# Half of w_in moved into the last stage, a first token block of 512, and a new attention order in a fused attention and soft-MoE kernel

## The chip, the cores and the metric

One core of a Trainium2 chip runs the whole program in one launch. The metric is the device time of one execution in microseconds, as the median over runs. The profile shows one further execution, and its own time is given beside its span.

## The reference

```python
attn = softmax(rmsnorm(q) @ rmsnorm(k).T / 8) @ v      # 4 batches, 12 heads, 448 tokens, 64 wide
x = attn as [1792, 768]
logits = x @ phi                                       # phi [768, 32]: 8 experts of 4 slots
d = softmax(logits, over tokens); slot_input = d.T @ x # [32, 768]
slot_out[e] = relu(slot_input[e] @ w1[e]) @ w2[e]      # w1 [8, 768, 1024], w2 [8, 1024, 768]
x = softmax(logits, over slots) @ slot_out             # [1792, 768]
h = x @ w_in                                           # w_in [768, 2048], float64 in memory
out = (h * sigmoid(1.702 * h)) @ w_out                 # w_out [2048, 768], float64 in memory
```

## The kernel before

The kernel has three stages.

**Attention.** 24 pairs of heads pass through a pipeline whose steps are listed with `op(name, engine, cost, due, function, needs, ...)`. `run` is a planner: it plays the list with its costs and emits each engine's instructions in the order that comes out. Where several steps of one engine could start at the same time, the one with the smallest due goes first. `SHIFT` adds a number to the due of each kind of step, and the strings in `ON` say for each pair whether a step runs on VectorE (D), GpSimd (P) or ScalarE (A). While attention runs, 24 pieces of expert weights are loaded ahead (`early`). They fill seven tiles of 128x3072: `NW` = 3 of `wpool`, which are loaded again later, and 4 that lie in `wi`, the place of the decoded w_in, and are not. At the end of attention five more tiles are filled (`ev`, `e0` to `e3`).

**Experts.** Eight experts follow each other. For each one TensorE computes `hps` = siT x w1 (line 1121, six steps of kk), VectorE applies the ReLU (`hs`, line 1134), TensorE turns it (line 1144), VectorE copies it into `hTz` (lines 1149, 1150), and TensorE multiplies it by w2 into `so_ps` (line 1154, eight steps of f, for the first six experts). A tile of weights that has been used is filled again with the next one of the list `stream` (`reload`, on SyncE's queue). From the sixth expert on `warm_b` adds dummy products. In the second expert `combine_turn` prepares the combine weights; for the first batch it also keeps a plain copy `c0` for the first tokens. After each step of the loops `win_turn` may decode one chunk of w_in: 24 chunks of 128x512 float64 values, 0.524 MB each, are loaded by ScalarE's queue (`win_load`, line 1043) and turned into float32 by `decode64` with two steps on ScalarE (lines 147, 150) and two on VectorE (line 144). The w2 of the last two experts come last in `stream` and are used by `last_mm` (line 1232). `u_step` (line 1261) multiplies their sum `before` by w_in, which gives `u`, the 32 slots' values in all 2048 features.

**Last stage.** Tokens are worked off in blocks, and a planner orders it too. For each of 16 feature tiles f, `f_mm` spreads `ust` to the tokens (line 1310), ScalarE applies Silu (`gg`, line 1318) and rounds it (`gh`, line 1327), VectorE takes the rest (`gl`, line 1332), and TensorE adds three products for each token tile of 128 and each half of 768 columns into `Y`: gh x wh, gh x wl, gl x wh (line 1351; in the first block line 1368). `us_mm` (line 1291) makes `ust` from `u` in four parts. In the first block the 16 tiles of w_out are loaded, decoded and split into `wh` and `wl` as well (lines 144 to 158, 1210, 1214). The blocks are 384, 384, 384, 384 and 256 tokens; `y_out` and `y_store` write a finished block.

Of the kernel before, what the change touches and what calls it, by code (L numbers as in the profile page):

```python
# [20 lines left out]
def soft_moe_block_kernel(  # L21
# [29 lines left out]
    NW, NWR, NW2 = 3, 4, 2  # L51
# [3 lines left out]
        gain="PDPDPDDDPDDPDPDPDDPDDDDD",  # L55
        qn="DPPDPPPPPPDPPPDPPPPPDPDD",
        kn="DPDDDPPPPPDDPPDPPPDDPDPP",
        qlo="PPDPPPDPDDPPDDPPDPDDPPPD",
        klo="DDDDDDPPPDPDDPDDDPDPDPDD",
        q2="PPDAAADAPDDDDDAAAAPDPPDA",  # L60
        k2="DDDADDADADPDADAAADPAADPA",
        e01="PPDPDPDPPPPPDDDPDDDPDPDP",
        e02="PPDPPPPPPDDDPPPPDDDDDPPD",
        e11="DPPPDDPPPPDDDPDDDDDDPDPP",
        e12="PPDDDPPPPDPDDPPDDDPPDDPD",
        x0="DDDDAAADADDDDAADAADAADDA",
        x1="DAAAADDAADADDADAADDADAAA",
        nr="DPPDPDPPDPDP",
# [96 lines left out]
    wi = wi_ctx.__enter__().tile([128, KD * DFF], F32, name="wi")  # L165
# [55 lines left out]
    for i, tag in enumerate(("ssq", "y0", "nt")):  # L221
# [42 lines left out]
        e0=4065.4, e1=1871.6, e2=705.9, e3=1336.9, early=76.2, esum=1946.8, ev=1170.2, exp=938.3, gain=3568,  # L264
        guard=-7.4, invert=-243.4, k2=1786.8, khi=-2180.8, klo=-680.2, kn=1837.3, lastlg=-2574.3, lk=1816.2,
        lk2=3100.6, logits=522.6, lq=1423.8, lq2=582.8, max=1121.1, meansq=1101.5, mx=-29, out=798.9,
        pe_tka=-2476.8, pe_tkb=3670.2, pe_tqa=681.5, pe_tqb=-366.9, pv=510.7, q2=1966, qhi=3834, qlo=1235.4,
        qn=1990.6, r_add=3872.4, r_back=3899.1, r_eb=1801, r_exp=-2634.4, r_fade=1302.1, r_gather=624.9,
        r_max=1791.5, r_more=-2250.9, r_neg=1305.5, r_old=1619.3, r_turn=681.3, r_z=352.5, recip=1344.9,
        sc=586, square=-471.5, squarek=473, ssb=-536.7, sumT=1332.9, sums=-8.9, tka=-2650.5, tka0=719.8,  # L270
        tkb=3875.6, tkb0=-229.5, tqa=-2002, tqa0=523.6, tqb=-542.8, tqb0=1302.7, v=4133.3, w_back=1921.6,
        w_copy=1410.9, w_exp=1561, w_guard=-358.8, w_max=-206.5, w_neg=-343.2, w_recip=-2399.9, w_scale=1149.9,
        w_sel=3867.1, w_sum=581.9, w_turn=1912.7, w_z=3874.4, x=2168.9, xmul=1473.5,
# [385 lines left out]
    for p in range(NP):  # L659
# [40 lines left out]
        if p >= NPE:  # L700
            op(("tka", p), "SP", 1.32, t - 16.3, lambda p=p: turn(p, "kt", KT, kk_t), sub("klo", "k2"), ("kt", p), [("ka", p)])
# [256 lines left out]
    left += [f for i in range(4) for f in place(wi[:, 3072 * i:3072 * (i + 1)], None)]  # L958
# [19 lines left out]
    with tc.manual_schedule():  # L978
# [26 lines left out]
        for h in range(2):  # L1005
# [23 lines left out]
            for i in range(6)  # L1029
# [17 lines left out]
        def win_turn():  # L1047
# [20 lines left out]

        def combine():
# [11 lines left out]
        def combine_turn(b):  # L1081
# [25 lines left out]
        c0 = bp.tile([NS, SF], F32, name="c0")  # L1107
# [61 lines left out]
        QU = DFF // 4  # L1169
# [3 lines left out]
        FB = dict(h=2, hs=2, wr=5, wf=4, gg=3, gh=4, gl=4, o=3, y0=1, y1=1, y2=1)  # L1173
# [19 lines left out]
        def w_step(f, i, h):  # L1193
# [3 lines left out]
            decode64(wf[f][:, c], wr[f][:, 2 * c.start:2 * c.stop], f % 2)[i]()  # L1197
# [58 lines left out]
        def u_step(kk):  # L1256
            if kk == 0:
                st["u"] = ps_o.tile([128, QU], F32, tag="o", name="u")
            for j in range(4):
                a = kk * DFF + j * QU  # L1260
# [10 lines left out]

        def u_hi():
            nc.scalar.activation(out=uh, in_=st["u"], func=AF.Copy)

        def u_lo():
            nc.vector.tensor_tensor(out=ul, in0=st["u"], in1=uh.bitcast(F32), op=ALU.subtract)

        def close():
# [4 lines left out]
            cp["ust"] = poolf("us", 1).tile([128, DFF], F32R, name="ust")  # L1283
            for t in FB:
                if t not in cp and t[0] not in "hy":
                    cp[t] = poolf(t + "_q", FB[t] - 3 * (t in right))

        def us_mm(j):
            st["us", j] = ps_h.tile([128, 512], F32, tag="h", name="f")
            for hl, t in ((0, uh), (1, ul)):  # L1290
                nc.tensor.matmul(
                    st["us", j], selu[:, j, hl].rearrange("p t s -> p (t s)"), t, start=(hl == 0), stop=(hl == 1)
                )
# [237 lines left out]
```

## Time and profile before

| what | value |
|---|---|
| median of 3 runs | 690.77 us (690.19 to 692.08) |
| the profiled execution's own time | 688.41 us |
| its span, first to last instruction | 686.6 us |
| TensorE busy | 617.3 us (90%) |
| VectorE busy | 396.3 us (58%) |
| ScalarE busy | 364.3 us (53%) |
| GpSimd busy | 164.5 us (24%) |

PE is TensorE, PEld its weight loads, DVE VectorE, ACT ScalarE, POOL GpSimd, SP SyncE; a q behind the name is the queue that issues transfers. L1154 is line 1154 of the kernel. The shares are means over the three stages, which have different limits, so they have to be read stage by stage.

### The profile page before, as it was taken

Reading aid. Unit: us, or ns where it says so; the run is one execution under the profiler, and the core shown is the slowest. Engines: PE = TensorE matmul, PEld = TensorE weight load, DVE = VectorE, ACT = ScalarE, POOL = GpSimd, SP = SyncE. Lnnn points to the kernel's source line nnn. Section 1 sums busy time; section 2 is a strip of 40 time slices with the busy share of each in tenths; the row PEclk is TensorE's granted clock in tenths of the full one; section 3 lists DMA queues with packets and bytes.
Section 4 is the critical chain, followed back from the end, with each engine's and each line's share of the span. In section 5 each row is a group of like instructions: output and inputs, shape, how many; then the busy total and the mean of one; then the engine's idle time right before and its main releaser. Section 6 shows DMA issues by size and latency. Waiting matters only on the chain.

```text
span 686.6 us, 10997 instructions
## 1 busy us (share of the span) xinstructions
PE 617.3 (90%) x4104; PEld 414.0 (60%) x4104; DVE 396.3 (58%) x657; ACT 364.3 (53%) x756; POOL 164.5 (24%) x193
## 2 busy tenths in 40 slices
PE   2989998999999999986743999999999999999997
PEld 1434343344444343453421344999899999999997
DVE  5978988898899997354444514899401211211211
ACT  4757787769768675643334412897413323432432
POOL 4565775873562551300000200000000000000000
PEclk9999999999999999999876999999999999999999
DMA  8989999998999999689899994761100100100101
GB/s 215 289 162 209 194 198 206 183 181 184 194 185 190 210 227 214 209 321 353 322 407 405 406 349 178 266 232 72 70 1 0 70 1 1 70 0 1 70 1 46
DMA packets 150965, 121.73 MB, mean 177 GB/s; under 512 B 106848, under 2 KB 131680, under 8 KB 150912
## 3 DMA queue, kind: packets, MB, share of 16 engines
q1 hardware_dynamic: 147824, 110.91, 59.7%
q10 hardware_dynamic: 3024, 10.03, 3.8%
q8 instruction: 32, 0.52, 0.3%
q14 instruction: 21, 0.17, 0.1%
q0 software_dynamic: 64, 0.10, 0.1%
HBM read 92.18 MB, written 5.51 MB: 142 GB/s over the span
## 4 chain that ended last, share of the span: by engine, by line
PE 67%; DMA 12%; DVE 11%; ACT 4%; issue 3%; POOL 3%; SPq 1%; ACTq 0%; DVEq 0%; POOLq 0%
PE y L1351 27%; PE y L1368 7%; PE sc L545 6%; PE pv L564 4%; PE so_ps L1154 4%; DVE wr L534 3%; DMA wr<-wr 3%; PE mx L529 2%; DMA wr<-in_q_dram 2%; PE h L1121 2%; PE f L1310 2%; DMA wr<-in_moe_w_dram 2%; DVE wr L417 1%; PE t L1113 1%; PE pv L559 1%
## 5 line engine op out<-in xcount | busy, mean ns | idle before, releaser
L1332 DVE TENSOR_TENSOR gl<-gg,gh 128x384 fp32r<-128x384 f32 (+1 forms) x80 | 42.2, 530 | 154.0 <-ACT gh L1327 153.2
L534 DVE TENSOR_REDUCE wr<-mx 128x2 f16<-128x896 f32 x92 | 99.8, 1085 | 16.1 <-PE mx L529 16.0
L1318 ACT ACTIVATE gg<-f 128x384 f32<-128x384 f32 (+1 forms) x78 | 36.4, 468 | 116.8 <-PE f L1310 115.4
L1351 PE MATMUL y<-wo,gh 128*128 128x384 f32 x352 | 75.3, 335 | 0.0
L549 ACT ACTIVATE e<-sc,esc 128x448 f32<-128x448 f32 x96 | 58.0, 642 | 12.2 <-PE sc L545 8.8
L1351 PEld LDWEIGHTS y<-wo,gh 128*128 128x128 f32 x352 | 62.1, 188 | 0.0
L552 POOL TENSOR_TENSOR es<-es,e 128x448 f32<-128x448 f32 x36 | 44.1, 1236 | 50.6 <-PE pv L564 31.6
L545 PE MATMUL sc<-wr 128*128 128x448 f16 (+1 forms) x192 | 49.0, 365 | 2.2 <-DMA wr<-wr 1.7
L1327 ACT ACTIVATE gh<-gg 128x384 fp32r<-128x384 f32 (+1 forms) x78 | 39.3, 504 | 16.3 <-PE y L1351 10.7
L1351 PE MATMUL y<-wh,gl 128*128 128x384 f32 x176 | 46.8, 337 | 0.0
L1351 PE MATMUL y<-wh,gh 128*128 128x384 f32 x176 | 46.7, 336 | 0.0
L1351 PE MATMUL y<-wl,gh 128*128 128x384 f32 x176 | 46.7, 336 | 0.0
L549 ACT ACTIVATE es<-sc,esc 128x448 f32<-128x448 f32 x54 | 33.5, 642 | 21.6 <-PE sc L545 21.4
L1351 PE MATMUL y<-wo,gl 128*128 128x384 f32 x176 | 44.8, 335 | 0.0
L412 ACT ACTIVATE wr<-wr 128x512 f32<-128x512 f32 x48 | 30.6, 644 | 15.8 <-DMA wr<-in_k_dram 4.8
L472 POOL TENSOR_TENSOR wr<-wr 128x512 f32<-128x512 f32 x31 | 34.6, 1134 | 11.6 <-DVE wr L448 7.8
L545 PEld LDWEIGHTS <-wr 128*128 128x128 f16 (+1 forms) x256 | 19.0, 103 | 30.1 <-issue 21.3
L147 ACT ACTIVATE wi<-wst 128x512 f32<-128x512 f32 x24 | 16.2, 674 | 36.5 <-DMA wr<-in_moe_w_dram 16.1
L144 DVE SCALAR_TENSOR_TENSOR wst<-wst 128x512 uint32<-128x512 uint32 x24 | 16.6, 690 | 29.2 <-ACT wst L150 27.3
L1351 PEld LDWEIGHTS y<-wl,gh 128*128 128x128 f32 x176 | 32.0, 188 | 0.0
L1351 PEld LDWEIGHTS y<-wh,gl 128*128 128x128 f32 x176 | 32.0, 188 | 0.0
L1351 PEld LDWEIGHTS y<-wo,gl 128*128 128x128 f32 x176 | 31.9, 188 | 0.0
(264 smaller groups left out, 1324.6 us busy)
## 6 DMA issues: line engine op xcount, KB each, us to landing
wr<-in_moe_w_dram SPq DMA_DIRECT2D x30, 512.0 KB, 8.8
wt<-in_moe_w_dram SPq DMA_DIRECT2D x24, 512.0 KB, 7.8
wr<-in_moe_w_out_dram SPq DMA_DIRECT2D x15, 768.0 KB, 4.3
wst<-in_moe_w_in_dram ACTq DMA_DIRECT2D x19, 512.0 KB, 6.9
wt<-in_moe_w_dram SPq DMA_DIRECT2D x20, 384.0 KB, 7.8
wr<-in_moe_w_dram SPq DMA_DIRECT2D x20, 384.0 KB, 5.7
out_dram<-o SPq DMA_DIRECT2D x13, 384.0 KB, 2.3
wr<-in_k_dram SPq DMA_DIRECT2D x11, 384.0 KB, 5.1
```

What stands on the lines that cost most here:

```text
L412: nc.scalar.activation(out=sqt[p][:, 8 * i:8 * i + 8], in_=rows(p, i), func=AF.Square, scale=D ** -0.5)
L472: eng.tensor_tensor(out=n, in0=n, in1=r.to_broadcast([P, 8, D]), op=ALU.mult)
L534: nc.vector.tensor_reduce(out=lanes(of(qb_t, p), 1)[:m, h:h + n, c, 0:1], in_=MX.pop((p, g))[:m, :n, :S], axis=AX.X, op=ALU.max,)
L545: nc.tensor.matmul(out, cols(a, n, c), cols(b, n), start=first, stop=not first)
L549: nc.scalar.activation(out=E[p, h, c], in_=SC.pop((p, h, c)), func=AF.Exp, scale=esc)
L552: on(f"e{h}{c}", p)[0].tensor_tensor(out=E[p, h, 0], in0=E[p, h, 0], in1=E[p, h, c], op=ALU.add)
L564: nc.tensor.matmul(PV[p][h * D:(h + 1) * D, :], t[:, 6 * n + 3 * h + c], E[p, h, c], start=(c == 0), stop=False)
L1318: nc.scalar.activation(out=ggt[w][:, :w[1]], in_=src[:, :w[1]], func=AF.Silu, scale=1.702)
L1327: nc.scalar.activation(out=gh[:, :w[1]], in_=ggt[w][:, :w[1]], func=AF.Copy)
L1332: nc.vector.tensor_tensor(out=G[w][1][:, :n], in0=ggt[w][:, :n], in1=G[w][0][:, :n].bitcast(F32), op=ALU.subtract)
L1351: nc.tensor.matmul(Y[t, u][:, :384], a[:, ts], b[f][:, u * 384:(u + 1) * 384], start=(f == 0 and i == 0), stop=(f == KF - 1 and i == 2),)
L1368: nc.tensor.matmul(Y[t, u][:, :384], a[:, t * 128:(t + 1) * 128], b[:, u * 384:(u + 1) * 384], start=(f == 0 and j == 0), stop=(f == KF - ...
```

## The change

- Only the first 1024 columns of w_in (12 chunks) are loaded and decoded in the experts' stage, one each 5.2 turns from turn 21 on, four loaded ahead at the start and then three ahead. `wi` is half as large; in the place that comes free `wpool` has five tiles instead of three.
- The other 1024 columns (groups g = 2 and 3, six chunks each) are loaded by SyncE's queue in the last stage, decoded into `wx` by the same four steps (`late_load`, `late_step`), multiplied by a kept copy of `before` (`late_u`) and split (`late_hi`, `late_lo`). `us_mm` for parts 2 and 3 works from these.
- Blocks are 512, 512, 384 and 384 tokens. The columns of `Y` are divided as 512 + 256; the 256-column parts of two token tiles share one bank, which a product with zeros opens (`y_tile`).
- In w_out, four of 16 tiles instead of eight take the decode with three VectorE steps (`f % 4`). Rings: wr 5 to 4, wf 4 to 3, gg 3 to 2, gl 4 to 3.
- All strings of `ON` and numbers of `SHIFT` are new, and `SHIFT` also has kinds of the last stage. The planner's cost of the step `tka` is 2.9 instead of 1.32.

```diff
-    NW, NWR, NW2 = 3, 4, 2
+    NW, NWR, NW2 = 5, 4, 2
-        gain="PDPDPDDDPDDPDPDPDDPDDDDD",
+        gain="DDPDDDDDPDDDDDDDDPDDDDPD",
...
-        if is_kept[key] is not None and nstream[0] < len(stream) - (0 if is_kept[key] else NW):
+        if is_kept[key] is not None and nstream[0] < len(stream) - (0 if is_kept[key] else 3):
...
-    wi = wi_ctx.__enter__().tile([128, KD * DFF], F32, name="wi")
+    wi = wi_ctx.__enter__().tile([128, KD * DFF // 2], F32, name="wi")
...
-    left += [f for i in range(4) for f in place(wi[:, 3072 * i:3072 * (i + 1)], None)]
+    left += [f for i in range(2) for f in place(wi[:, 3072 * i:3072 * (i + 1)], None)]
...
-        NC, NWI = 512, KD * DFF // 512
+        NC, NWI = 512, KD * DFF // 1024
...
-            kc, col = divmod(j * NC, DFF)
+            kc, col = j // 2, j % 2 * NC
...
-            if j < NWI and g >= 16 + 2.75 * j:
-                if 0 < j < NWI - 4:
-                    win_load(j + 4, nc.scalar)
+            if j < NWI and g >= 21 + 5.2 * j:
+                if 0 < j < NWI - 3:
+                    win_load(j + 3, nc.scalar)
...
-        for j in range(5):
+        for j in range(4):
             win_load(j, nc.sync)
...
-        QU = DFF // 4
+        QU = DFF // 8
...
-        FB = dict(h=2, hs=2, wr=5, wf=4, gg=3, gh=4, gl=4, o=3, y0=1, y1=1, y2=1)
+        FB = dict(h=2, hs=2, wr=4, wf=3, gg=2, gh=4, gl=3, o=3, ws=2)
...
-            decode64(wf[f][:, c], wr[f][:, 2 * c.start:2 * c.stop], f % 2)[i]()
+            decode64(wf[f][:, c], wr[f][:, 2 * c.start:2 * c.stop], f % 4)[i]()
...
+        def late_load(g, kk):
+            st["ws", g, kk] = cp["ws"].tile([128, 2 * NC], U32, tag="ws", name="ws")
+            nc.sync.dma_start(
+                out=st["ws", g, kk], in_=win64[kk * 128:(kk + 1) * 128, 2 * g * NC:2 * (g + 1) * NC]
+            )
+
+        def late_step(g, kk, i):
+            a = kk * NC
+            decode64(cp["wx"][:, a:a + NC], st["ws", g, kk], True)[i]()
+
+        def late_u(g):
+            st["lu", g] = ps_h.tile([128, 512], F32, tag="h", name="f")
+            for kk in range(KD):
+                for j in range(4):
+                    a = kk * NC + 128 * j
+                    nc.tensor.matmul(
+                        st["lu", g][32 * j:32 * j + 32, :128], keep[:, kk % 2, kk // 2], cp["wx"][:, a:a + 128],
+                        start=(kk == 0), stop=(kk == KD - 1),
+                    )
...
+            parts, n = ((uh, ul), QU) if j < 2 else ((st["luh", j], st["lul", j]), 128)
+            for i in range(512 // n):
+                r = i + 2 * j if j < 2 else i
+                for hl, t in enumerate(parts):
+                    nc.tensor.matmul(
+                        st["us", j][:, i * n:(i + 1) * n], selu[:, r, hl].rearrange("p t s -> p (t s)"), t,
+                        start=(hl == 0), stop=(hl == 1),
+                    )
...
+        YC = (slice(0, 512), slice(512, DM))
+
         def y_tile(t, u):
-            ps, tag = (ps_c, "c") if t < 2 else ((ps_t, "t"), (ps_o, "o"))[u]
-            Y[t, u] = ps.tile([128, 512], F32, tag=tag, name="y")
+            if u == 0:
+                Y[t, 0] = ps_c.tile([128, 512], F32, tag="c", name="y")
+            elif t % 2 == 0:
+                ps, tag = ((ps_t, "t"), (ps_o, "o"))[t // 2]
+                pair = ps.tile([128, 512], F32, tag=tag, name="y")
+                Y[t, 1], Y[t + 1, 1] = pair[:, :256], pair[:, 256:]
+
+                some = ident.bitcast(F16).rearrange("p (o f) -> p o f", o=1).to_broadcast([128, 2, 256])
+                nc.tensor.matmul(pair, zeros, some, start=True, stop=False)
...
-                    Y[t, u][:, :384], a[:, ts], b[f][:, u * 384:(u + 1) * 384],
-                    start=(f == 0 and i == 0), stop=(f == KF - 1 and i == 2),
+                    Y[t, u], a[:, ts], b[f][:, YC[u]], start=(f == 0 and i == 0 and not u),
+                    stop=(f == KF - 1 and i == 2 and (u == 0 or t % 2 == 1 or (t + 1) * 128 == w[1])),
...
-        blocks = [(t0, min(384, NT - t0)) for t0 in range(0, NT, 384)]
+        blocks = [(0, T0), (T0, 512), (T0 + 512, 384), (T0 + 896, 384)]
...
-                        [("fhi", w), ("flo", w)] + ([("y", (w[0], n, f - 1), t)] if f else []),
+                        [("fhi", w), ("flo", w)] + ([("y", (w[0], n, f - 1), t)] if f else [("yo", prev, i, u) for i in (t, t1) if i < prev[1] // 128 for u in range(2)]),
```

## Rows read from the trace of the kernel before

**Rows 1.** Busy time by stage (us, instructions), then granted clock, DMA share, GB/s.

```profile
core 0: us, PE busy (x) PEld busy (x) DVE busy (x) ACT busy (x) POOL busy (x), PEclk, DMA share, GB/s
45.00:302.10 257.10, 243.75 (x1423) 104.85 (x1423) 215.66 (x325) 184.66 (x418) 133.58 (x129) 1.00 0.94 203
302.10:330.10 28.00, 21.43 (x255) 11.66 (x255) 14.34 (x37) 11.60 (x23) 0.57 (x2) 0.94 0.90 334
330.10:379.60 49.50, 25.97 (x296) 13.02 (x299) 22.71 (x40) 19.34 (x33) 0.00 (x0) 0.72 1.02 398
379.60:408.00 28.40, 26.97 (x277) 9.77 (x270) 8.86 (x20) 7.27 (x17) 3.93 (x17) 1.00 1.05 379
...
429.60:487.20 57.60, 57.19 (x315) 56.52 (x316) 51.85 (x71) 48.07 (x78) 0.00 (x0) 0.97 0.46 167
489.85:682.50 192.65, 192.62 (x1111) 192.30 (x1110) 36.49 (x70) 61.35 (x129) 0.00 (x0) 1.00 0.07 25
```

**Rows 2.** Waits from 330 to 380 us: total us, times, longest.

```profile
PE t L1144 <- DVE hTz L1149: 22.7, 3, 11.1
```

**Rows 3.** Timeline of ScalarE and VectorE before the fifth expert's ReLU.

```profile
360.80 0.69 ACT L147 ACTIVATE wi<-wst 128x512 f32<-128x512 f32 x1 [7.13 <-DMA wr<-in_moe_w_dram]
...
372.16 0.69 DVE L144 SCALAR_TENSOR_TENSOR wi<-wi,wst 128x512 uint32<-128x512 uint32 x1
372.77 0.48 DVE L1134 TENSOR_SCALAR hs<-h,rz 128x256 f32<-128x256 f32 x1
```

**Rows 4.** DMA traffic in 322 to 333, 333 to 360, 395 to 413 us.

```profile
DMA packets 670, 2.46 MB, mean 224 GB/s; under 512 B 69, under 2 KB 69, under 8 KB 670
...
DMA packets 3277, 10.91 MB, mean 404 GB/s; under 512 B 365, under 2 KB 365, under 8 KB 3275
...
DMA packets 6109, 6.31 MB, mean 351 GB/s; under 512 B 194, under 2 KB 6000, under 8 KB 6108
```

**Rows 5.** Waits of SyncE's queue from 295 to 420 us.

```profile
SPq L115 <- PE so_ps L1154: 10.2, 1, 10.2
```

**Rows 6.** Timeline of TensorE in the experts' stage (start, duration).

```profile
327.64 1.93 PE L1154 MATMUL so_ps<-wr,hTz 128*32 128x256 f32 x24
...
336.87 5.12 PE L1154 MATMUL so_ps<-wr,hTz 128*32 128x256 f32 x45 [0.28 <-DVE hTz L1150]
...
373.30 0.69 PE L1144 MATMUL t<-ident,hs 128*128 128x128 f32 x2 [11.07 <-DVE hTz L1149]
...
380.32 0.50 PE L1113 MATMUL t<-ident 128*128 128x256 f16 x3
```

**Rows 7.** Timeline of TensorE: the last products of the last experts.

```profile
422.33 1.08 PE L1232 MATMUL h<-wr,hTz 128*32 128x128 f32 x32
```

**Rows 8.** Timeline of TensorE in the last stage: starts of 512, 384, 256 columns.

```profile
439.02 0.39 PE L1291 MATMUL f<-uh,selu 128*128 128x512 f32 x1
439.25 0.40 PE L1291 MATMUL f<-ul,selu 128*128 128x512 f32 x1
...
530.33 0.51 PE L1351 MATMUL y<-wh,gh 128*128 128x384 f32 x2
530.67 0.51 PE L1351 MATMUL y<-wl,gh 128*128 128x384 f32 x2
...
660.36 0.28 PE L1310 MATMUL f<-cT,ust 128*128 128x256 f32 x1
660.48 0.87 PE L1351 MATMUL y<-wo,gh 128*128 128x384 f32 x4
```

**Rows 9.** Costliest groups of the whole run: busy us, mean ns.

```profile
L1332 DVE TENSOR_TENSOR gl<-gg,gh 128x384 fp32r<-128x384 f32 (+1 forms) x80 | 42.2, 530 | 154.0 <-ACT gh L1327 153.2
L1318 ACT ACTIVATE gg<-f 128x384 f32<-128x384 f32 (+1 forms) x78 | 36.4, 468 | 116.8 <-PE f L1310 115.4
...
L1327 ACT ACTIVATE gh<-gg 128x384 fp32r<-128x384 f32 (+1 forms) x78 | 39.3, 504 | 16.3 <-PE y L1351 10.7
...
L147 ACT ACTIVATE wi<-wst 128x512 f32<-128x512 f32 x24 | 16.2, 674 | 36.5 <-DMA wr<-in_moe_w_dram 16.1
L144 DVE SCALAR_TENSOR_TENSOR wst<-wst 128x512 uint32<-128x512 uint32 x24 | 16.6, 690 | 29.2 <-ACT wst L150 27.3
```

More of the change, by code (lines that the diff above doesn't have):

```diff
@@ L263, in soft_moe_block_kernel @@
     SHIFT = dict(
[L264 to L268, printed above, removed]
@@ new lines, in soft_moe_block_kernel @@
+        early=-1419, esum=885.5, ev=761, exp=630.4, f=-203.2, fhi=4764.1, flo=-1087.4, gain=3345.6,
+        guard=2335.6, invert=-973.2, k2=740.7, keep=602.1, khi=-1227.2, klo=-1190.9, kn=3318.5, lastlg=2716.8,
+        ld=6.4, lh=-323.3, lk=21, lk2=-590.7, ll=-2003.2, logits=-1444.9, lq=-163.4, lq2=-1275.1, lu=-1084.1,
+        lw=-368.5, lx=119.1, max=-652.9, meansq=-556.9, mx=-1056, out=-329.1, p=-180.8, pa=-212.5, pc=-131.2,
+        pe_tka=-579.6, pe_tkb=1463.7, pe_tqa=1489.8, pe_tqb=-1455.5, pt=-2097.5, pv=-480.7, q2=1791.9,
@@ L1028, in soft_moe_block_kernel @@
             w2ctx.enter_context(tc.tile_pool(name=f"wst{i}", bufs=1, reuse_waits="tile", side="right"))
-            for i in range(6)
+            for i in range(5)
         ]
@@ L1259, in u_step @@
             for j in range(4):
[L1260 removed]
+                a = kk * DFF // 2 + j * QU
                 nc.tensor.matmul(
@@ L1283, in close @@
             cp["ust"] = poolf("us", 1).tile([128, DFF], F32R, name="ust")
+            cp["wx"] = poolf("wx", 1).tile([128, KD * NC], F32, name="wx")
+            cp["lu"] = poolf("lu", 1).tile([128, 2, 2, 128], F32R, name="lu")
             for t in FB:
-                if t not in cp and t[0] not in "hy":
+                if t not in cp and t[0] not in "hy" and FB[t] > 3 * (t in right):
                     cp[t] = poolf(t + "_q", FB[t] - 3 * (t in right))
@@ new lines, in soft_moe_block_kernel @@
+        work = [(t0, n, f) for t0, n in blocks for f in range(KF)]
+        TB = 1.1
+        for g in (2, 3):
+            u = 24 + 16 * TB * g
+            for kk in range(KD):
+                op(
+                    ("lw", g, kk), "SP", 1.4, u - 24 + 2.3 * kk, lambda g=g, kk=kk: late_load(g, kk), ["close"], ("ws", g, kk),
+                )
+                for i in range(4):
+                    act = i < 2
+                    op(
+                        ("lx" if act else "ld", g, kk, i), "ACT" if act else "DVE", 0.6 if act else 0.62,
+                        u - 20 + 2.3 * kk + 0.5 * i, lambda g=g, kk=kk, i=i: late_step(g, kk, i),
+                        [("lw", g, kk)] + [("lu", 2)] * (g == 3) if not i else [("lx" if i < 3 else "ld", g, kk, i - 1)],
+                        None, [("ws", g, kk)] * (i == 3),
+                    )
+            op(("lu", g), "PE", 2.5, u - 5, lambda g=g: late_u(g), [("ld", g, kk, 3) for kk in range(KD)], ("h", "lu", g))
+            op(("lh", g), "ACT", 0.25, u - 4.5, lambda g=g: late_hi(g), [("lu", g)])
+            op(("ll", g), "DVE", 0.25, u - 4.2, lambda g=g: late_lo(g), [("lh", g)], None, [("h", "lu", g)])
@@ L1414, in soft_moe_block_kernel @@
         for j in range(4):
             op(
-                ("us", j), "PE", 0.43, 18 + 12 * j, lambda j=j: us_mm(j), ["uh", "ul"] + ([("y", (0, 384, 4 * j - 3), 2)] if j else []), ("h", "us", j),
-            )
-            op(("usc", j), "DVE" if j % 2 else "ACT", 0.6, 18.5 + 12 * j, lambda j=j: us_copy(j), [("us", j)] + ["close"] * (j == 0), None, [("h", "us", j)])
-        blocks = [(t0, min(384, NT - t0)) for t0 in range(0, NT, 384)]
-        work = [(t0, n, f) for t0, n in blocks for f in range(KF)]
@@ L1423, in soft_moe_block_kernel @@
+        op("keep", "DVE", 0.25, 6, lambda: nc.vector.tensor_copy(out=keep, in_=before), [("u", KD - 1)])
+        op("close", "POOL", 0, 8, close, ["keep"] + [("f", w) for w in work[:2]] + [("cT", b) for b in range(B)])
         for f in range(KF):
-            d = 24 + TF * f
+            d = 24 + 4 * TB * f
             first = 20 if f == 0 else 0
@@ L1439, in soft_moe_block_kernel @@
                 for i in range(3):
-                    act = f % 2 and not i
+                    act = f % 4 and not i
                     op(
```

144 lines of the change are left out of this document (83 added, 61 removed).

## The prediction

> **What bounds the kernel now.** I read the busy time by stage first. Attention (45 to 302 us) keeps TensorE busy 243.75 of 257.1 us. In the experts' stage it is busy 25.97 of 49.5 us between 330 and 380 us, at a mean granted clock of 0.72, that is, partly at 1.2 and partly at 2.4 GHz. From 429.6 us on, in the last stage, it is busy all the time: 57.19 of 57.6 us in the first token block, 192.62 of 192.65 in the others [rows 1]. So the first and last stages are bound by TensorE, and the middle one by something else. The waits of 330 to 380 us say by what: TensorE waits 22.7 us, in three waits, for the copy into hTz [rows 2], which follows the ReLU (`hs`) on VectorE. The timelines of VectorE and ScalarE show why that is late: `hs` starts at 372.77 us, right behind the joins of a w_in chunk, and ScalarE, which starts a chunk, had waited 7.13 us for a load [rows 3]. Both engines work in program order, so one late w_in chunk holds the ReLU of an expert whose own weights are there. The transfers are late because the DMA is full, at 404 GB/s on average from 333 to 360 us. Before that it ran at 224 GB/s from 322 to 333 us [rows 4], where SyncE waited 10.2 us for TensorE to free a buffer [rows 5]. That is 11 us in which 11 x 0.404 - 2.46 = 2.0 MB more could have come: 4.9 us lost.
>
> **The experts' stage, by TensorE.** The edit takes 12 of 24 w_in chunks, with their loads and decodes, out of this stage, spreads the others over 5.2 turns instead of 2.75, and keeps five reloadable weight buffers instead of three. From 330.1 to 379.6 us TensorE was idle 49.5 - 25.97 = 23.5 us [rows 1]. It also ran slowly: 45 products took 5.12 us where 24 at full clock took 1.93 [rows 6], so 5.12 - 45 x 0.080 = 1.5 us per expert and 3 experts = 4.5 us. From 28 us of waste I leave 5 us for the handover ReLU, transposes and copy, which no edit touches: about 23 us to gain. In 302.1 to 330.1 us TensorE idles 6.6 us [rows 1]; chunks now start at turn 21, in the second half of the second expert, so its ReLU has no decode before it: 3 us more, less about 1 us for the extra transposes and copies of c0. By TensorE the stage could end 25 us earlier, at 383 instead of 408 us. The last three experts (379.6 to 408 us) keep their 28.4 us, as TensorE is busy 26.97 of it, part with dummy products that stay in the code [rows 1, 6].
>
> **The same by the DMA.** Taken away: 12 x 0.524 MB = 6.29 MB, at 404 GB/s 15.6 us. The gap of 4.9 us closes, since w1 and w2 loads no longer wait for the third expert: two more buffers become free in the first two experts. The w_out and last w2 tiles, which run at 351 GB/s [rows 4], keep their time. So the last expert tile lands some 20.5 us earlier; the small packets of those tiles end at about 413 us now, then at 392.5. It is used from 422.33 us on [rows 7], and the chain, moved by 25 us, asks for it at 397. The DMA therefore does not hold TensorE, but with only 4 us of slack. I let the first product of the last stage come 25 us earlier, plus 1 us for the `u` products with half the columns, at 403.6 us instead of 429.6: 26 us gained. Bounds: 15.6 us if only the bytes count, and 31 if all of 28 us and 3 us go.
>
> The Trainium skill (DMA: Bandwidth & Descriptors, "Where 436 GB/s comes from") puts loads from HBM at about 358 GB/s per core. This trace disagrees, with 404 GB/s sustained [rows 4], and the measurement decides; by the page the bytes would be worth 17.6 us instead of 15.6.
>
> **The last stage's products.** A token tile's 768 columns become 512 + 256 instead of 384 + 384, with as many instructions. Starts of 384-column products are 0.34 / 2 = 0.17 us apart (0.173 as a mean over the later blocks: 192.65 us less 10.3 of `f`, by 1056), those of 512 columns 0.23, and the 256-column `f` product is followed after 0.12 us [rows 8], its successor's full weight load included. A pair costs 0.23 + 0.12 = 0.35 instead of 0.346 us, equal within the rounding of the rows: over 14 x 16 x 3 = 672 pairs 0, with 0.005 x 672 = 3 us on both sides. The `f` products, 32 of 512 and 32 of 384 columns for 64 of 384 and 16 of 256, cost the same 13 us. Eight bank-opening zero products at no more than 0.23 us: +1.8 us. Later `us` products in 128-column pieces, 16 at no more than 0.12 instead of 4 at 0.23: +1.0 us. `late_u` is 48 products of 128 columns, of which 32 take about 1.08 us [rows 7]: +1.6 us. In sum +4.4 us on TensorE.
>
> **The first block.** It has 512 tokens, so its 57.6 us grow by the 128 tokens' own cost, which the later blocks lose: 192.65 us for 11 tiles [rows 1] is 17.5 us a tile. So 75 us, at no net cost. Into it go the 12 chunks. VectorE gets 24 joins x 0.69 = 16.6 us, and `gl` 16 x 0.53 / 3 = 2.8 us: 51.85 + 19.4 = 71 us. ScalarE gets 24 x 0.674 = 16.2 us, `gg` and `gh` a third more (16 x (0.468 + 0.504) / 3 = 5.2 us), and four decode steps moved from VectorE, under 1.01 us each: 48.07 + 25.4 = 73.5 us [rows 1, 9]. TensorE needs 75 us and some of the 4.4 us above, say 77. Hence the decodes hide behind TensorE, with 4 to 6 us of cover; before, cover was 57.6 - 51.85 = 5.8 us. If it is gone, every us of ScalarE or VectorE costs one. The rings for wr, wf, gg and gl lose one buffer each, and group 2 must be decoded before feature tile 8; I add 1 us of stalls. The bounds are 0 and 16.6 us (nothing of the late decode hidden). The loads, 6.29 MB in 77 us beside w_out, ask for 82 GB/s where 167 flow [rows 1].
>
> **Transitions and end.** One block less. A tile pair now shares a bank, so a block's first tile waits for the copies of two tiles; behind the second tile come one or two more tiles of 1.05 us, which cover two copies of about 0.5 us. At the end the last store is 256 columns instead of 384. I take 0 for both, -0.5 to +2.
>
> The Trainium skill (PSUM — Partial Sum Buffer, "PSUM bank collisions raise a hardware error") forbids a read of a bank while TensorE writes its other half. If each of the 8 pairs then made TensorE wait for one 0.5 us copy, that would add 4 us, and the sum would be 674 instead of 670 us; no row of this trace shows a shared bank. I give it 1 in 10, within the forecast's own range.
>
> **Attention.** The steps dealt to engines change: without the tiny `nr` steps VectorE has 4 fewer, GpSimd 1 more, ScalarE 3 more. VectorE (215.66 of 257.1 us) and GpSimd (133.58) have room, and TensorE idles 13.4 us [rows 1]. The order by kind is new as well. It could give at most those 13 us; the nearest size for a loss is the same. No row says which way, so I take 0, with -7 to +7 in the range. The early loads stay 24 pieces.
>
> **Sum.** 688.41 us (span 686.6) - 26 + 4.4 + 1 + 0 = 667.8 us; the median of the runs stands 2.36 us above the profiled execution (690.77 - 688.41), so 670 us.
>
> **Rivals.** (a) Only the bytes count: the ReLU still sits behind chunks, whose loads are issued three ahead instead of four. The gain is 15.6 us, and the time 670 + 10.4 = 680 us. For it: the DMA stays full, so a chunk still queues behind expert tiles. Against: a lead of 3 x 5.2 = 15.6 turns, formerly 11. (b) The first block starves: ScalarE's 73.5 us in 77 leave little, and an in-order queue that is behind makes TensorE wait. With all 16.6 us exposed in place of the 1 us, 670 + 15.6 = 686 us. Against: VectorE ran at 90% of its time in the same block before, with TensorE at 99%. (c) Attention moves by about 7 us: 663 or 677 us. (d) Slower: the 256-column product is held by its neighbour's weight load. If each cost as much as one of 384, a pair would be 0.402 us, +0.052 x 672 = 35 us: 705 us. It decides from 0.031 us more a product (21 us). Against: the 0.12 us behind the `f` product [rows 8]; for it, that `f` is one product among 13, and here it is every second one.
>
> **How the numbers follow.** Forecast 0.60, with its own range 663 to 677; (a) 0.13; (b) 0.11; (c) 0.06 for each sign; (d) 0.04. The time is the forecast's, 670 us. The range is 659 to 684: it holds the forecast, most of (a), half of (b) and both of (c). A measurement of this kernel can tell about 0.3%, 2 us, from no change. (d) and the far end of (b) with (a) together are slower: 0.05; between them and the rest, 0.03 within; faster 0.92.
>
> **What would show it.** In the changed profile: the first `y` product at about 404 us; TensorE's idle time before the transposes behind hTz down from 22.7 to under 6 us; no dip of the DMA at 320 to 335 us; a first block of 75 to 80 us with ScalarE over 90% busy; 256-column products 0.12 us before their successor. It is wrong if `hs` still waits behind chunks for loads, if TensorE waits in the first block for `gh`, `gl` or the late `us`, or if attention ends elsewhere than at 302 us.

## The result and the profile after

The changed kernel took 670.74 us in the median of four runs (669.10 to 675.14); the kernel before took 690.48 beside it. The ratio is 0.973, with a 95% interval of 0.967 to 0.979. The profiled execution of the changed kernel took 671.69 us, its span 669.9 us; before it was 688.41 and 686.6 us.

By stage the two profiled executions differ so (us; a stage runs from its first TensorE product to the next stage's first, read from the timelines of TensorE; the product with zeros that opens a bank is not counted as the first):

| | before | after | difference | predicted |
|---|---|---|---|---|
| attention ends (first product of the experts' stage) | 304.43 | 299.52 | -4.9 | 0 (-7 to +7) |
| experts' stage, to the first `y` product | 125.18 | 99.88 | -25.3 | -26 |
| last stage, to the end of the span | 257.0 | 270.5 | +13.5 | +5.4 |
| span | 686.6 | 669.9 | -16.7 | -20.6 |

The forecast of 670 us is off by 0.74 us, but not because every term was right. The middle stage did what the prediction says. Beside it stand 4.9 us of gain that it did not count and 8.1 us of loss (13.5 - 5.4) that it priced too low. That these two nearly cancel is luck: the profiled execution is 671.69 - 667.8 = 3.9 us above the sum. The rest is luck too: the median lies 0.95 us below the profiled execution this time, where it lay 2.36 us above it before.

The rows by stage, as in [rows 1], of the changed kernel (busy us and instructions by engine, granted clock, DMA share, GB/s; attention, experts, first token block, later blocks):

```profile
core 0: us, PE busy (x) PEld busy (x) DVE busy (x) ACT busy (x) POOL busy (x), PEclk, DMA share, GB/s
45.00:299.40 254.40, 246.35 (x1455) 107.22 (x1455) 216.82 (x317) 186.46 (x414) 139.41 (x146) 0.99 0.94 207
299.40:399.40 100.00, 85.68 (x1095) 43.07 (x1093) 34.64 (x89) 28.06 (x53) 4.17 (x20) 1.00 1.01 375
399.40:486.50 87.10, 82.04 (x523) 70.48 (x524) 72.31 (x97) 70.24 (x111) 0.00 (x0) 0.96 0.53 182
487.10:664.90 177.80, 177.79 (x1009) 155.13 (x1008) 30.88 (x56) 53.92 (x101) 0.00 (x0) 1.00 0.07 25
```

The experts' stage now keeps TensorE busy 85.68 of 100 us at full clock, where between 330 and 380 us it had been busy half the time at 0.72 [rows 1]. The first block is the odd one: 87.1 us, of which TensorE is idle 5.06, and a granted clock of 0.96. In the later blocks TensorE has no hole.

Waits of TensorE in the experts' stage (us in total, times, longest), to be read against [rows 2]:

```profile
PE t L1159 <- DVE hTz L1164: 3.1, 6, 0.6
PE h L1136 <- DMA wt<-in_moe_w_dram: 1.3, 6, 0.3
PE h L1136 <- DMA wr<-in_moe_w_dram: 1.3, 3, 0.8
```

The wait for hTz, 22.7 us in three pieces before, is 3.1 us in six short ones of 0.6 us at most. Beside it there are now waits for the weights themselves. The chain that ended last says that from 336 to 374 us, and again from 386 to 394 us, the transfers set this stage's pace (start, us, what):

```profile
335.81 11.37 DMA wr<-in_moe_w_dram
...
347.25 7.58 DMA wr<-in_moe_w_dram
...
354.89 8.97 DMA wt<-in_moe_w_dram
363.93 10.27 DMA wt<-in_moe_w_dram
...
386.25 7.71 DMA wr<-in_moe_w_out_dram
```

Products of the last token tiles, as in [rows 8], with 512 and 256 columns:

```profile
662.08 0.40 PE L1417 MATMUL y<-wh,gl 128*128 128x512 f32 x1
662.31 0.28 PE L1417 MATMUL y<-wh,gh 128*128 128x256 f32 x1
662.43 0.28 PE L1417 MATMUL y<-wl,gh 128*128 128x256 f32 x1
```

A 256-column product is followed after 0.12 us, a 512-column one after 0.23, with a full weight load before each. The pair costs 0.35 us as forecast, and rival (d) is out. The later blocks bear it out over their whole length: ten tiles in 177.8 us are 17.8 us a tile, against 17.5 of eleven tiles before, and these 2.7 us are within the 3 us that were allowed.

TensorE's waits in the first block, and below them ScalarE's for the late chunks:

```profile
PE y L1434 <- ACT gh L1383: 2.6, 2, 2.1
PE y L1434 <- ACT wo L1225: 1.4, 1, 1.4
PE y L1434 <- ACT wh L1225: 1.1, 1, 1.1
PE y L1434 <- ACT gh L1379: 0.8, 1, 0.8
```

```profile
ACT wx L147 <- DMA ws<-in_moe_w_in_dram: 5.9, 7, 1.4
```

All that TensorE waits for comes from ScalarE, and ScalarE itself is held 5.9 us by late w_in chunks. They take 3.8 to 8.1 us from issue to landing on SyncE's queue, behind loads of raw w_out, in two buffers.

### The profile page after: what moved, and what is told of

Same layout as the page of the kernel before. It is cut to its first block, busy times and chain, and to the rows that moved or that the text cites. A ratio compares the mean times of both kernels' runs of the same rounds, so it can differ in the third digit from the quotient of the medians.

```text
span 669.9 us, 11244 instructions
## 1 busy us (share of the span) xinstructions
PE 620.4 (93%) x4227; PEld 389.9 (58%) x4227; DVE 389.8 (58%) x628; ACT 364.8 (54%) x727; POOL 169.3 (25%) x210
## 4 chain that ended last, share of the span: by engine, by line
PE 55%; DMA 17%; DVE 10%; ACT 7%; issue 4%; POOL 3%; SPq 2%; DVEq 0%; ACTq 0%; POOLq 0%
PE y L1417 25%; PE sc L549 5%; PE pv L568 5%; DMA ws<-in_moe_w_in_dram 4%; PE y L1434 4%; DMA wt<-in_moe_w_dram 4%; DMA wr<-wr 3%; DMA wr<-in_moe_w_dram 3%; DVE wr L538 3%; PE mx L533 2%; PE pv L563 2%; PE so_ps L1169 2%; DMA wr<-in_k_dram 1%; PE f L1366 1%; PE h L1136 1%
## 5 line engine op out<-in xcount | busy, mean ns | idle before, releaser
L1388 DVE TENSOR_TENSOR gl<-gg,gh 128x512 fp32r<-128x512 f32 (+1 forms) x64 | 39.9, 624 | 141.4 <-PE y L1417 125.8
L1417 PE MATMUL y<-wo,gh 128*128 128x512 f32 x320 | 69.9, 340 | 0.0
L1417 PE MATMUL y<-wh,gl 128*128 128x512 f32 (+1 forms) x160 | 42.9, 339 | 0.0
L1417 PE MATMUL y<-wl,gh 128*128 128x512 f32 (+1 forms) x160 | 42.8, 338 | 0.0
L1417 PE MATMUL y<-wh,gh 128*128 128x512 f32 (+1 forms) x160 | 42.7, 338 | 0.0
L1417 PE MATMUL y<-wo,gl 128*128 128x512 f32 (+1 forms) x160 | 41.0, 337 | 0.0
L1434 PE MATMUL y<-wo,gh 128*128 128x512 f32 (+1 forms) x128 | 27.4, 360 | 4.8 <-ACT gh L1383 2.6
L421 DVE TENSOR_REDUCE wr<-wr 128x16 f32<-128x1024 f32 x24 | 29.1, 1211 | 4.7 <-ACT wr L416 4.7
L556 POOL TENSOR_TENSOR wr<-wr,e 128x448 f32<-128x448 f32 x19 | 23.1, 1219 | 21.5 <-PE pv L568 14.8
L556 DVE TENSOR_TENSOR es<-es,e 128x448 f32<-128x448 f32 x35 | 25.7, 745 | 4.3 <-PE pv L568 2.4
```

The costliest lines, as they stand in the source:

```text
L556: on(f"e{h}{c}", p)[0].tensor_tensor(out=E[p, h, 0], in0=E[p, h, 0], in1=E[p, h, c], op=ALU.add)
L1388: nc.vector.tensor_tensor(out=G[w][1][:, :n], in0=ggt[w][:, :n], in1=G[w][0][:, :n].bitcast(F32), op=ALU.subtract)
L1417: nc.tensor.matmul(Y[t, u], a[:, ts], b[f][:, YC[u]], start=(f == 0 and i == 0 and not u), stop=(f == KF - 1 and i == 2 and (u == 0 or t % ...
L1434: nc.tensor.matmul(Y[t, u], a[:, t * 128:(t + 1) * 128], b[:, YC[u]], start=(f == 0 and j == 0 and not u), stop=(f == KF - 1 and j == 2 an ...
```

## The experiments

My theory after this reading was: the experts' stage lost its 25 us because both its bounds left together, the bytes and the in-order work; attention gained by its order; and the first block is 10 us too long because ScalarE, working in order, is held by late chunks. The rivals to it are told run by run. All ratios are to the kernel before, timed beside each; where no other is named, the kernel changed is the changed kernel. Stage times are from one profiled execution each. What each run gave by stage (us):

```
                       attention  experts'  first   span   median  ratio [95%]
                       ends       stage     block
kernel before           304.43    125.18    57.60   686.6
changed kernel          299.52     99.88    87.10   669.9  670.74  0.973  [0.967, 0.979]
no late chunks          299.25     99.16    77.60   659.4  661.57  0.960  [0.958, 0.963]
late decode, no load    299.11     99.87    83.70   666.0  668.47  0.970  [0.968, 0.972]
late load, no decode    298.38     98.54    85.56   665.8  667.57  0.969  [0.966, 0.971]
loads' time planned     297.97    105.18    88.01   674.5  676.33  0.980  [0.977, 0.983]
three chunk buffers     297.24    100.05    91.06   671.7  674.17  0.981  [0.975, 0.987]
loads from GpSimd       301.12    103.94   105.12   693.5  690.15  1.002  [1.000, 1.005]
order refitted          299.94     99.82    86.97   670.4  672.21  0.976  [0.972, 0.979]
old attention order     305.06     98.80    87.85   675.1  677.60  0.984  [0.980, 0.988]
two tiles not reused    300.96    103.19    86.68   674.2  676.29  0.983  [0.979, 0.988]
before, new attention   298.58    126.95    57.62   682.5  684.33  0.992  [0.990, 0.995]
before, half the loads  303.63    121.66    57.60   682.3  684.87  0.995  [0.992, 0.997]
before, half decodes    304.34    123.01    57.58   684.3  685.76  0.995  [0.993, 0.998]
```

**1. No late chunks.** The ops `lw`, `lx` and `ld` are gone, and `late_u` reads a constant.

```diff
-        op(("lw", g, kk), "SP", 1.4, ...)
-        op(("lx" if act else "ld", g, kk, i), ...)
+            nc.gpsimd.memset(cp["wx"], 0.001)
```

> The changed kernel without the late half of w_in: the twelve late loads and their 48 decode instructions are left out, and the columns are filled with a constant, so the second half of the hidden columns is wrong. The late products of u and all else stay. My theory is that the first block's 86.9 us hold some 10 us that come from these chunks (idle TensorE of about 5 us behind ScalarE, and the lower clock after it): the first block falls to 75 to 78 us and the time to 659 to 663. The rival is that the block is long from what the new first product, the zero products and the y order cost on TensorE: then the block stays above 84 us and the time above 668.

The block took 77.60 us and the time fell to 661.57 us: the theory. This is also the figure that the prediction gave for TensorE alone ("say 77"). Windows of the first block, of this kernel and below of the changed one in five pieces:

```profile
398.40:476.00 77.60, 77.59 (x523) 67.74 (x524) 56.56 (x74) 56.94 (x87) 0.00 (x0) 1.00 0.36 123
```

```profile
399.40:411.40 12.00, 12.00 (x61) 10.38 (x62) 9.90 (x13) 11.30 (x18) 0.00 (x0) 0.86 0.68 250
411.40:423.40 12.00, 10.65 (x60) 9.02 (x59) 11.18 (x16) 9.45 (x16) 0.00 (x0) 1.00 0.74 244
423.40:435.40 12.00, 9.40 (x49) 7.78 (x48) 10.42 (x15) 10.82 (x18) 0.00 (x0) 0.94 0.82 272
435.40:447.40 12.00, 12.00 (x106) 10.40 (x106) 11.37 (x17) 10.38 (x17) 0.00 (x0) 0.92 0.74 263
447.40:486.50 39.10, 38.00 (x256) 32.90 (x255) 29.45 (x41) 28.29 (x45) 0.00 (x0) 1.00 0.27 90
```

The same 523 products keep TensorE busy 77.59 us here and 82.04 us there. So the 9.5 us that the late chunks add are 5.06 us of idle TensorE and 4.45 us of longer busy time, most of it at a lower granted clock (by the mean of 0.96, 0.04 x 87.1 = 3.5 us). Finer windows of the changed kernel show where: TensorE pauses half of 430 to 433 us, and the clock is 0.65 and 0.78 in the next six us, that is, partly at 1.2 GHz; it is all at 1.2 GHz (0.50) from 400 to 403 us, behind a stretch of 2.16 us busy in 3. Not every pause does this: behind 2.01 us busy in 3 from 421 us on the clock stays at 1.00, and in run 1 it does so behind 2.17 us busy from 397 to 400 us.

```profile
397.00:400.00 3.00, 2.16 (x6) 0.84 (x5) 1.16 (x4) 2.97 (x5) 0.00 (x0) 0.96 0.77 261
400.00:403.00 3.00, 3.00 (x9) 2.42 (x9) 2.18 (x4) 3.00 (x5) 0.00 (x0) 0.50 0.61 252
...
421.00:424.00 3.00, 2.01 (x11) 1.74 (x12) 2.83 (x4) 1.76 (x4) 0.00 (x0) 1.00 0.79 298
424.00:427.00 3.00, 2.47 (x15) 2.00 (x14) 2.27 (x4) 3.00 (x6) 0.00 (x0) 1.00 0.94 294
...
430.00:433.00 3.00, 1.47 (x9) 1.09 (x7) 2.39 (x4) 2.96 (x6) 0.00 (x0) 1.00 0.87 264
433.00:436.00 3.00, 2.46 (x8) 2.02 (x8) 2.96 (x6) 2.52 (x4) 0.00 (x0) 0.65 0.67 212
436.00:439.00 3.00, 3.00 (x53) 2.47 (x53) 2.54 (x5) 2.52 (x5) 0.00 (x0) 0.78 0.66 218
```

**2. Late decodes without their loads.** `late_step` reads two constant tiles.

```diff
-            st["ws", g, kk] = cp["ws"].tile([128, 2 * NC], U32, tag="ws", name="ws")
-            nc.sync.dma_start(out=st["ws", g, kk], in_=win64[...])
+            st["ws", g, kk] = st["wz"][kk % 2]
```

> The changed kernel with all 48 late decode instructions, but none of the twelve late loads: they decode two constant tiles, so the late columns are wrong, and no instruction of theirs waits for a transfer. If the waits for the late loads are what ScalarE loses (it waits 5.9 us for them, and it works in order), most of the loss goes: block 77 to 80 us, time 662 to 665. If the work itself is too much for ScalarE and VectorE in this block, nearly nothing changes: 669 to 671.

**3. Late loads, without their decodes.** One copy of 8 columns per chunk in place of the four decode steps.

```diff
+            nc.scalar.activation(
+                out=cp["wx"][:, a:a + 8], in_=st["ws", g, kk][:, 1:16:2].bitcast(F32), func=AF.Copy, scale=2.0 ** -112
+            )
```

> The changed kernel with all twelve late loads, but in place of each chunk's four decode instructions a single copy of 8 columns by ScalarE, which waits for the load as the first decode did; the late columns are otherwise a constant. If the waits cost the time, it stays near the changed kernel: 666 to 671. If the work costs it, the time falls to 659 to 663. Since a buffer now comes free at once, the waits are shorter than in the changed kernel, so something between would mean that the buffers' return is part of it.

Neither expectation held as a split. The work alone makes the block 83.70 us, 6.1 more than without chunks; the loads alone 85.56 us, 8.0 more; both together 9.5 more. Each by itself carries most of the loss. These are single executions; by the medians the work alone costs 6.9 us (668.47 - 661.57) and the loads alone 6.0 (667.57 - 661.57), so which of the two weighs more is not shown. A window of run 2 shows the work's side, with VectorE and ScalarE busy 11.86 and 11.83 of 12 us; a window and a wait row of run 3 show the loads' side, with ScalarE busy only 6.55 of 12 us:

```profile
411.00:423.00 12.00, 11.65 (x67) 9.97 (x66) 11.86 (x17) 11.83 (x19) 0.00 (x0) 1.00 0.34 126
```

```profile
408.90:420.90 12.00, 10.21 (x50) 8.70 (x49) 8.01 (x10) 6.55 (x14) 0.00 (x0) 0.86 0.80 279
```

```profile
ACT wx L1310 <- DMA ws<-in_moe_w_in_dram: 9.2, 6, 3.1
```

**4. The loads' time told to the planner.**

```diff
     QUEUE = dict(
+        raw=(2.2, 3), lw=(1.5, 3),
```

> The changed kernel with one thing more in the planner's table of transfer times: the raw w_out loads are given 2.2 us on the queue and 3 us to landing, the late w_in loads 1.5 and 3 us, where before it counted only 1.35 us after the issue. Work, bytes, buffers and queue are the same; only the order of the instructions in the last stage changes. If ScalarE's order was fitted to loads that land too early, the first block loses its idle TensorE: 79 to 83 us, time 663 to 668. If two buffers and the decode's work set the pace, the time stays within 2 us of 671 or becomes worse.

The first theory missed: the block stays at 88.01 us, and the time becomes worse. The experts' stage is 5.3 us longer, since ScalarE now starts the first two pieces of w_out at 395.92 and 398.49 us, behind a step of `u`, where it started them at 393.07 and 393.98 us.

**5. Three buffers for the late chunks,** and three for raw w_out.

```diff
-        FB = dict(h=2, hs=2, wr=4, wf=3, gg=2, gh=4, gl=3, o=3, ws=2)
+        FB = dict(h=2, hs=2, wr=3, wf=3, gg=2, gh=4, gl=3, o=3, ws=3)
```

> The changed kernel with three buffers for the late chunks in place of two, and three for raw w_out in place of four, so that both fit. If the late chunks' return of buffers sets the pace, ScalarE's waits for them fall below 3 us and the block to 82 to 85 us: time 666 to 669. If raw w_out needs its fourth buffer as much, or the work fills ScalarE and VectorE anyway, it stays at 669 to 674.

ScalarE's wait for chunks fell from 5.9 to 2.9 us, as the first theory asked, but the block grew to 91.06 us and the time, 674.17 us, is what the other theory says; ScalarE waits 3.8 us for raw w_out instead:

```profile
ACT wf L147 <- DMA wr<-in_moe_w_out_dram: 3.8, 3, 1.3
ACT wx L147 <- DMA ws<-in_moe_w_in_dram: 2.9, 3, 1.3
```

**6. The late loads on GpSimd's queue.**

```diff
-                    ("lw", g, kk), "SP", 1.4, ...
+                    ("lw", g, kk), "POOL", 4.0, ...
-            nc.sync.dma_start(
+            nc.gpsimd.dma_start(
```

> The changed kernel with the twelve late loads issued by GpSimd on its own queue, no longer in order behind the 768 KB loads of w_out on SyncE's queue; in the planner each is given 4 us. Buffers, bytes and decodes are the same. If the late loads are late because of the queue ahead of them (3.8 to 8.1 us to landing), they land in 3 to 5 us, ScalarE waits less for them and the first block falls to 81 to 85 us, the time to 665 to 669. If two buffers and full engines set the pace, it stays at 669 to 673.

The loads did land sooner, 4.3 us in the median against 5.5, but the block took 105.12 us and the time is 690.15 us, which neither theory allowed: TensorE waited 15.8 us for ScalarE's w_out copies. The 4 us that the planner was given per load, one after the other, also reordered the rest, so this run says nothing against the queue by itself.

```profile
PE y L1434 <- ACT wo L1225: 15.8, 3, 6.7
```

**7. The order alone, refitted.** The planner counts the loads' time (from the fourth w_out load on), and 19 shifts are refitted to it.

```diff
+        raw=(2.1, 2), lw=(1.4, 2),
...
+    SHIFT.update(
+        abs=40.7, act=46.2, f=-195.7, fhi=-19.8, flo=-2307.7, ld=-139.3, lh=-36.2,
+        ll=-1230.8, lu=-2442.4, lw=31.7, lx=-19.1, raw=125.3, us=-240.2, usc=-50.2,
+        wd=42.9, whi=44.5, wlo=35.0, y=-194.4, close=-47.5,
+    )
```

> The changed kernel with nothing but another order of the last stage's instructions: the planner counts 2.1 us on the queue and 2 us to landing for a raw w_out load (from the fourth on) and 1.4 and 2 us for a late w_in load, and the shifts of nineteen last-stage steps are refitted to that. Work, bytes, buffers, queues and the attention stage's order are the changed kernel's. If the 9.5 us that the late chunks add to the first block are mostly a matter of order (ScalarE held by loads that have not landed while products wait for its gh), the block falls from 87.1 to 80 to 84 us, and the time to 662 to 667, faster than both kernels. If they are the work on two full engines, which the decodes without any load (83.7 us) and the loads without decodes (85.6 us) would each still show, the block stays above 85.5 us and the time at 669 to 674.

The theory lost: 86.97 us and 672.21 us, the changed kernel's within the interval. Yet the order did what it was for, since ScalarE's wait for chunks fell to 1.9 us:

```profile
ACT wx L147 <- DMA ws<-in_moe_w_in_dram: 1.9, 3, 1.1
```

TensorE lost as much elsewhere. The first stretch has a pause for a w_out copy, from 406 us on, and the clock falls behind it:

```profile
406.00:409.00 3.00, 0.84 (x6) 0.41 (x4) 2.97 (x5) 3.00 (x6) 0.00 (x0) 1.00 1.00 419
409.00:412.00 3.00, 2.79 (x10) 2.42 (x11) 2.97 (x5) 2.79 (x5) 0.00 (x0) 0.63 0.44 125
```

By runs 2, 5 and 7 ScalarE's wait for a late chunk is not the only cause, though by run 3 it is enough to cost about as much. What fits the runs with decodes is that the late chunks bring the two engines so near to full in the first 48 us that, whichever step comes last there (a `gh`, a w_out copy, a chunk), TensorE pauses for it. That is argued from these rows; no run shows it alone.

**8 and 9. Attention's order.** Run 8 is the changed kernel with the old attention letters and shifts; run 9 the kernel before with nothing but the new ones.

```diff
-        op(("tka", p), "SP", 2.9, ...          # run 8; run 9 the other way round
+        op(("tka", p), "SP", 1.32, ...
```

> The changed kernel with the attention stage's order put back: the engine letters, the shifts of the attention steps and the planner's cost of one transposing transfer are those of the kernel before; the last stage's shifts stay. If the 4.75 us that the attention stage gained come from the refitted order, the first product of the experts starts at 303.5 to 305.5 instead of 299.7, and the time is 674.5 to 676.5. If they come from the other tiles that the attention stage loads early (five expert tiles and half of w_in's space), it stays at 670 to 672.

> The kernel before with nothing of the change but the attention stage's order: engine letters, shifts of the attention steps, planner's cost of one transposing transfer. If the order gains by itself, the experts' first product starts at 299 to 301 instead of 304.4 and the time is 684.5 to 687. If the order only pays together with the five early tiles, the time is 689 to 692, or worse, as the order was fitted to another list of loads.

Both times the order decides. Ten programs with the new order end attention at 297.24 to 301.12 us (mean 299.2), the four with the old one at 303.63 to 305.06 (mean 304.4), whatever tiles they load early. It is worth 5.2 us. Run 8's time, 677.60 us, is 1 us above what was expected of it; run 9's attention and time, 298.58 and 684.33 us, lie a little below. The timelines of TensorE of runs 8 and 9:

```profile
305.06 1.52 PE L1164 MATMUL h<-selw,pacc 128*128 128x32 f32 x12 [0.40 <-DVE zt L1005]
```

```profile
298.58 1.42 PE L1132 MATMUL h<-selw,pacc 128*128 128x32 f32 x12
```

**10 and 11. Half the loads, or half the decodes, of the kernel before.**

```diff
+            if j % 2:                      # run 10, in win_load
+                wraw[j] = wraw[j - 1]
+                return
...
+                if j % 2:                  # run 11, in win_turn, in place of decode64
+                    nc.gpsimd.memset(wi[:, j * NC:(j + 1) * NC], 0.001)
```

> The kernel before without half of w_in's loads: each odd chunk is decoded from the tile of the chunk before it, so half the columns are wrong; all 24 decodes stay, at their places. 6.3 MB of the experts' stage's transfers are gone. If the bytes bound the experts' stage, the 125.2 us fall by 6.3 MB / 404 GB/s = 15.6 us, to about 110, and the time to 673 to 677. If the in-order ReLU behind the chunks' decodes bounds it, nearly all stays: 686 to 690, and the waits of TensorE for hTz stay near 22 us.

> The kernel before with all 24 loads of w_in, but each odd chunk's decode replaced by a fill on GpSimd, so half the columns are wrong. Every byte still moves. If the bytes bound the stage, the time stays: 686 to 690. If the decode work ahead of the ReLU (with its waits for the chunks) bounds it, the waits for hTz fall under 12 us and the time falls by 8 to 16 us, to 674 to 682.

Neither alone moves the stage by more than 3.5 us; the times, 684.87 and 685.76 us, lie 1.1 and 0.2 us below the 686 to 690 us that were expected of a change that gains nearly nothing. TensorE's wait in the kernel before, then the window of the stage and the wait, first of half the loads, then of half the decodes:

```profile
PE t L1144 <- DVE hTz L1149: 23.5, 6, 11.1
```

```profile
303.60:425.30 121.70, 94.45 (x1078) 45.25 (x1078) 53.25 (x113) 43.20 (x78) 4.46 (x19) 0.89 0.83 306
```

```profile
PE t L1147 <- DVE hTz L1152: 17.5, 6, 7.7
```

```profile
304.30:427.30 123.00, 93.66 (x1077) 44.72 (x1077) 37.03 (x89) 28.65 (x54) 9.95 (x31) 0.88 0.96 354
```

```profile
PE t L1147 <- DVE hTz L1152: 19.2, 6, 8.6
```

Without half the loads the DMA has room (a share of 0.83), but the ReLU still sits behind 24 decodes. Without half the decodes the queue stays full (0.96), and ScalarE still waits 18.5 us before the first steps of the remaining decodes (16.1 in the kernel before). Over the whole stage the wait for hTz is 23.5 us in the kernel before; it stays at 17.5 and 19.2.

Neither run is a clean halving. In run 10 an odd chunk is decoded in the tile in which the even one has just been decoded, so ScalarE waits for VectorE there, which the kernel before does not show; half the loads alone may be worth more than 3.5 us.

```profile
ACT wst L150 <- DVE wi L144: 11.3, 10, 2.9
```

In run 11 the last expert's transposes start 401.65 - 304.34 = 97.3 us after the stage's start, 5.5 us sooner than before (407.23 - 304.43 = 102.8). Then 3.3 us are lost again: VectorE's copy for the last experts (line 1243) comes behind steps of w_out's decode, TensorE waits 1.9 us for it, and the next 16 `u` products take 3.50 us, where they took 1.92 before (the granted clock is 0.52 from 421 to 424 us). Up to there half the loads are worth 3.5 us (402.95 - 303.63 = 99.3) and half the decodes 5.5, still far from the 25.3 us of the change.

```profile
420.64 3.50 PE L1264 MATMUL u<-wi,before 128*32 128x512 f32 x16 [0.28 <-DVE before L1250]
```

```profile
424.51 1.92 PE L1261 MATMUL u<-wi,before 128*32 128x512 f32 x16 [0.28 <-DVE before L1247]
```

**12. Two of five weight tiles not loaded again.**

```diff
-    left = [f for _ in range(NW) for f in place(wpool.tile(...), True)]
+    left = [f for n in range(NW) for f in place(wpool.tile(...), True if n < 3 else None)]
```

> The changed kernel with two of its five tiles for expert weights used once only: they hold the first weights as now, but are not loaded again, so that three tiles (and the two others) pass the rest through, as in the kernel before. Bytes and decode work are those of the changed kernel. If the 25 us that the experts' stage lost come from the work that left it (6.3 MB and twelve decodes together), it stays at 99 to 103 us and the time at 670 to 674. If the buffers are what lets the loads run ahead, the stage is 107 to 122 us and the time 678 to 692.

The stage took 103.19 us, just above the first expectation and well below the second; the time, 676.29 us, lies between the two. So of 25.3 us some 3.3 come from the two further buffers, and 22 from the rest, which is above all the loads and decodes taken away together. The later start and slower pace of the chunks came with these, and were not tried apart.

## Why the prediction came out right

- **What bounds the experts' stage: right.** It said that the DMA and the in-order ReLU behind chunks both hold it. Runs 10 and 11 show that each alone gives back 2.2 to 3.5 us at the stage's end, and 5.5 at most in the experts. Rival (a), by which the stage gains the 15.6 us of the bytes and no more, is refuted by the measured 25.3, and run 10 shows that the bytes alone are not worth 15.6.
- **Experts' stage, -26 us: right,** measured -25.3. Of its two sums, the one by TensorE left 5 us for handovers, and 3.1 us remain as waits for hTz. The one by the DMA was wrong in its conclusion that the DMA does not hold TensorE and leaves it 4 us of slack: TensorE's waits for weights and the chain show that the transfers set the pace from 336 to 374 us, at 375 GB/s over the stage. The dip was to close; it is smaller, not gone: 355 GB/s on average from 317 to 333 us, with single slices near 200.
- **TensorE's extra products, +4.4 us: right in the sum, not in its parts.** Without late chunks, which leaves their `late_u` products in, the last stage runs from 398.41 to 659.4 us, 261.0 us, against 257.0 before: +4.0. But `late_u` was counted as 48 products, 1.6 us; the trace of run 1 has two such groups of 48 (the first is shown), 1.52 us each, 3.0 in sum. The other terms came out at 4.0 - 3.0 = 1.0 us instead of 4.4 - 1.6 = 2.8, so the sum is right in part by luck.

```profile
399.77 1.52 PE L1313 MATMUL f<-wx,keep 128*32 128x128 f32 x48
```

- **The first block, +1 us of stalls within 0 to 16.6: the term that was mis-sized.** Measured: 9.5 us. The step that failed is "the decodes hide behind TensorE, with 4 to 6 us of cover". The sums were right (VectorE 72.3 busy where 71 was said, ScalarE 70.2 where 73.5), but cover was counted over the whole block. The chunks are due before feature tiles 8 and 12, so the work is packed into the first part (their decodes run from 413 to 459 us). In the first 48 us VectorE is busy 42.9 and ScalarE 42.0 of 48 us, and in the last 39 us only 29.5 and 28.3. And pauses can cost more than their length: 5.06 us of idle time came with 4.45 us of longer busy time. This was rival (b) by its mechanism, at a little over half its price.
- **Attention, 0: a gain of 4.9 us.** Runs 8 and 9 give it to the order alone. It lay inside the bounds, and the prediction gave no reason for either sign.
- **Transitions and end, 0 (-0.5 to +2): right, with two small parts that cancel.** TensorE goes from the first block to the second without a wait, where before it waited 1.0 us for `gg`, and from then on the view of its waits is empty. From the end of the later blocks' window to the end of the span it is 669.9 - 664.9 = 5.0 us, formerly 686.6 - 682.5 = 4.1. The rule on shared banks (the Trainium skill, PSUM — Partial Sum Buffer, "PSUM bank collisions raise a hardware error") was priced at 4 us. The trace has no wait of TensorE for a copy of a shared bank in the later blocks, so here it cost nothing.
- **The DMA's rate.** The Trainium skill (DMA: Bandwidth & Descriptors, "Where 436 GB/s comes from") gives about 358 GB/s a core; the changed kernel sustains 406 GB/s from 333 to 360 us, as the kernel before did 404 [rows 4].

Of the signs that the prediction named, two of those of being wrong came: TensorE waits in the first block for `gh` (2.6 + 0.8 us), and attention ends earlier. The block takes 87.1 us with ScalarE busy 70.24 of them, 81%, where 75 to 80 us and over 90% were named.

What stays open: whether an order exists that brings the first block near its 77.6 us. Four ways were tried (runs 4 to 7) and none did; that the block could stay at 87 us while ScalarE's wait for chunks fell from 5.9 to 1.9 us shows that shortening this wait alone does not help, not that nothing does. In run 2 TensorE's busy time is 2.5 us longer than in run 1 at a granted clock of 1.00; the windows don't say why, and the ends of matmuls are modelled.

## What to carry to other kernels

Where two bounds lie close together, as the bytes and the in-order decodes did, relieving one gives little (2 to 4 us at the stage's end) and relieving both gives most of the gain (some 22 of 25 us); so work out the stage's end by each bound and take the later one. When work is moved under a busy engine, count the cover up to the moment the work is due, not over the whole stage, and allow, beside a pause of TensorE, for busy time that a lower clock may stretch after it. A forecast whose total is right may still hold two errors that cancel; only the stages show it.

## What the runs showed that I had not expected

- TensorE's pause of about 2 us from 430 to 436 us (6 - 1.47 - 2.46) lies beside six us at a granted clock of 0.65 and 0.78, that is, an estimated 3 x 0.35 + 3 x 0.22 = 1.7 us lost on top.
- Work without loads (+6.1 us) and loads without work (+8.0 us) do not add up to both (+9.5 us). Why not is not shown: in run 2 the two engines are nearly full, in run 3 ScalarE waits 9.2 us for loads.
- The end of attention varies by nearly 4 us (297.24 to 301.12) between profiled executions of programs whose attention has the same order, so one stage time alone is no proof there; ten against four is.
